# The last token row's MLP as a row of its own, and the row before it moved ahead, in a two-layer decode kernel

## The chip, the cores and the metric

The kernel runs on one core of one Trainium2 chip. The metric is the device time of one execution in microseconds. TensorE multiplies, VectorE and ScalarE move and compute, GpSimd does the reductions over partitions, SyncE (SP in the profile) issues all DMAs.

## The reference

Eight tokens (B = 8) of width D = 448 pass twice through an attention block (A) and an MLP block (B), with the same caches and weights both times:

```python
x = x + _A_ref(_layernorm(x), k_cache, v_cache, wq, wo)     # 16 query heads on 8 kv heads, Sk=4096, Dh=256
x = x + _B_ref(_layernorm(x), w1, w2, w3, w4)
x = x + _A_ref(_layernorm(x), k_cache, v_cache, wq, wo)
x = x + _B_ref(_layernorm(x), w1, w2, w3, w4)
# _A_ref: q = x @ wq; softmax(q k / 16) v per head; concatenated heads @ wo
# _B_ref: the first half shifts columns along the sequence. With one position (S = 1) its shifted
#         columns are all zero, so that half adds nothing:
#         x1 = x;  return x1 + gelu(_layernorm(x1) @ w3) @ w4,  F = 1792
```

Everything is in bfloat16. Each token row has its own K and V cache of 8 heads, 2 MB each for K and for V. One layer reads 268 MB of them; the two layers would read 537 MB, and the kernel keeps some of it on chip between the layers.

## The kernel before

**Work items.** The kernel is written as a list of operations, each with an engine, the data that it reads and writes, the PSUM banks that it uses, an estimated duration and a priority. `Plan.schedule` plays the list through a small model of the engines and fixes the order on each; `synchronise` adds the semaphore waits. Two rules of `Plan.op` matter here. An operation waits for the writers and readers of its data, and an operation that uses a bank waits for the last operations of the other engines on that bank, in the order in which the program was written. So everything that uses the shared bank `psM` keeps its written order where engines alternate. The priority is by default the place in the list; operations of `dv` and `pe` have it lowered by a million (`urge[0]` = `CH`) and so go first, unless `urge[0]` is set to 0. The planner's model of TensorE counts blocks of 128 instruction pairs (`fetched`, `BLOCK`), and fills expected idle time with dummy matmuls on the identity (`filler`, L1366 to L1377).

**Tiling.** K and V come from DRAM in quarters of 512 KB ("units"), each a slot `kv[:, slot*2048 ...]`; there are 30 slots. One DMA brings up to `most` neighbouring units (`next_kv`). It is issued when as many slots in a row are free. A K quarter is transposed on TensorE as f32 words (L1165, four 128 x 128 transposes per bank of `psT`, eight banks' worth per head) and copied back over itself by VectorE (L1148) or ScalarE (L1149).

**A head.** `front` does the 64 score matmuls of a head (L985, 16 per quarter, into `psM` columns 256 on), copies them to `sS` (L1004), finds the maximum, and takes the exponential on ScalarE (L1019) into `pT`. A K quarter's slot is free after its score matmuls. `back` loads V and multiplies `pT` with it: 32 matmuls of 128 x 2 weights against 256 columns, in four column groups of the array (L1050), into one of two banks `psP` by turns. VectorE copies the result in two bf16 parts to `oS` (L1064, L1066), four matmuls add the groups (L1074), L1080 divides by the sum into `oT`, and four matmuls with wo add the head to a row in `psR` (L1099). After a row's seventh head, that row is copied to `oW` in two parts (L1109, L1111) and turned into columns in `psM` ("turn", lines L927 and L930 of the helper `dup`), and L1123 adds x. The eighth head goes through wo directly in columns ("wo_mm", also L927 and L930), and L1135 writes the new x.

**Order of the rows.** Row b's second layer is woven with the first layer of row b + 1. Heads are kept or free: K of heads 3 to 7 stays on chip between the layers (head 7 half, the rest of it held in transposed form), V of head 7 and half of head 6. The rest is read twice. Heads 0, 1 and 2 are the free ones. The last row (b = 7) has no next row, and runs these tasks, "f" for `front` and "b" for `back`, with 6/0 for head 0 of row 6, which is finished here:

b 6/0, f 6, f 7, b 6/1, f 0, b 6, b 6/2, f 5, f 1, | b 7, f 4, f 2, b 5, f 3, b 4, b 3, b 0, b 1, b 2.

The bar is ours; the change refers to that place. After a front of the second layer the next head's query is computed (`second_queries`, L1220 and L1223, matmuls at L814), also on `psM`.

**MLPs.** `mlp` computes sums (L722) and moments, the inverse root by two Newton steps (L700 to L708), w3 as 56 matmuls (L830), gelu (L880, L891, L893, the tanh at L895 on ScalarE, L906 into `hT`), w4 as 70 matmuls in columns (`y_mm`, L927 and L930 through `dup`), and L919 adds the residual. It is used for each row's first layer, for rows 0 to 5 of the second layer together (in row 5, on a bank of `psT`), and for rows 6 and 7 of the second layer at the very end, with n = 2, on `psM`. `result` then turns the columns into rows (L1187), copies them (L1191) and writes them out (L1193).

Of the kernel before, what the change touches and what calls it, by code (L numbers as in the profile page):

```python
# [6 lines left out]
P = 128  # L7
B = 8
D = 448
# [16 lines left out]
AT = (-4, -3, -2)  # L26
MLP_ROW, MLP_AT, MLP_TO = 5, 3, 7
OUT_AT = 23.5
QLAST = 2
# [430 lines left out]
def bass_interleave_layers__gqa_block_cached__mixer_s_mlp__decode_kernel(  # L460
# [44 lines left out]
    ident_f = sb("ident_f", [P, P], f32)  # L505
    ident_b = sb("ident_b", [P, P], bf)
    xT = sb("xT", [P, NC5, B], bf)
# [4 lines left out]

    xf = sb("xf", [P, NC5, 4], bf)
    xoT = sb("xoT", [P, NC5, B], bf)
    acc = [sb(f"acc{i}", [P, NC5], f32) for i in range(2)]
# [14 lines left out]
    yb = sb("yb", [P, NC5, B], bf)  # L530
    q1T = sb("q1T", [P, B, 32], bf)
    q2T = [sb(f"q2T{i}", [P, 32], bf) for i in range(2)]
    cursor[0] = (cursor[0] + 31) // 32 * 32
# [10 lines left out]
    x_row = nc.alloc_sbuf_tensor_at("x_row", [B, NC5 * P], bf, offset=row0)  # L544
    o_row = nc.alloc_sbuf_tensor_at("o_row", [B, D], bf, offset=row0)
    assert row0 + 2 * NC5 * P <= hb0 + 4 * D
    NR, NO, NS = 6, 2, 2
# [29 lines left out]


    sems = {e: nc.alloc_semaphore(f"s_{e}") for e in ("pe", "dve", "act", "pool")}
    slot_sem = [nc.alloc_semaphore(f"s_slot{i}") for i in range(QUARTERS)]  # L580
# [55 lines left out]
    def const_a(gp):  # L636
        gp.memset(ident_f[:, :], 0.0)
        gp.memset(x_row[:, D:D + P], 0.0)
        gp.memset(mask[:, :], 1.0)
        gp.memset(x3T[:, :, :], 0.0)  # L640
        for t, c in [(t, 1) for t in x1c + x2c] + [(xf, 2)]:
            gp.memset(t[:, :, c:c + 1], 1.0)
            last = gp.memset(t[:, :, c + 1:c + 2], -1.0)
# [214 lines left out]
    WQ = ["wq0", "wq1", "wq2", "wqx0", "wqx1"]  # L858

    def mlp(src, skey, n, dst, dkeys):  # L860

# [22 lines left out]
        else:  # L884
# [11 lines left out]
                rd=["g2"], wr=["g1"], prio=urge[0] + len(plan.ops))  # L896
        for r in range(n) if few else ():

# [7 lines left out]
        dv(lambda v: v.scalar_tensor_tensor(hT[:, 0:m], a_, 1.0, h_, ALU.add, ALU.mult),  # L906
           rd=HB + ["g1"], wr=["hT"])

        def y_mm(t):
# [119 lines left out]
    def back(layer, b, h):  # L1029
# [40 lines left out]
        def sum_mm(t):  # L1070
            last = None
            for c in range(2):
                for w in range(2):
# [16 lines left out]
                             (x2c[b % 2][:, :, 0], ("x2", b),  # L1090
                              x3T[:, :, b] if b < B - 2 else xf[:, :, b - B + 2], ("x3", b)))
        ak = ("acc", layer)
# [32 lines left out]
        if k == HKV:  # L1125
            def wo_mm(t):
# [8 lines left out]
            dv(lambda v: v.tensor_tensor(xout, acc[layer][:, :], psM[:, YC:YC + NC5 * YW:YW], ALU.add),  # L1135
               rd=["psM", ak], wr=[ok] + (["x3all" if b < B - 2 else "xf"] if layer else []), banks=[M],
               name="acc", prio=hi)
# [38 lines left out]

    s_out = nc.alloc_semaphore("s_out")

    def result(n, at):
# [3 lines left out]
        def ot(t):  # L1183
            last = None
            for kc in range(4):
# [3 lines left out]
            return last  # L1189
        pe(ot, 4, rd=[("xo", at), "ident_b"], wr=[key], banks=[bk])  # L1190
        mark(dv(lambda v: v.tensor_copy(o_row[0:n, :], ps[0:n, :].bitcast(bf)[:, 0:D]), dur=0.5,  # L1191
           rd=[key], wr=["o_row", "hb", "g1", "g2", "hT"], banks=[bk]))
        plan.op("sp", lambda eng: eng.dma_start(out[at:at + n, 0, :], o_row[0:n, :]), 0.1, "out",  # L1193
                rd=["o_row", "hb", "g1", "g2", "hT"], wr=[("done", n)],
                dma=(s_out, 32 if at else 16), prio=loads[0] + (11.5 if at else OUT_AT))

# [56 lines left out]
    def first_queries():  # L1253
        def xt(t):
# [4 lines left out]
            return last  # L1259
        pe(xt, 4, rd=["xr0", "xr1", "xr2", "ident_b"], wr=["psM"], banks=[M])  # L1260
        dv(lambda v: v.tensor_copy(xT[:, :, :].rearrange("p a n -> p (a n)"),
# [79 lines left out]
    for b in range(B):  # L1341
# [23 lines left out]

    def filler(bank):  # L1366
# [5 lines left out]
        def warm(t):  # L1372
            return t.matmul(dst, ident_b[:, :], bcast(ident_b[:, 0:n // 4], 4, 1), start=True,  # L1373
                            stop=True)
        o = Op("pe", warm, (0.22 * n / 512, 0.43 * n / 512, n, 1), "warm", 0)
        o.deps[plan.writer["ident_b"]] = True
        return o  # L1377
# [5 lines left out]
    with nc.Block() as blk:  # L1383
# [48 lines left out]
```

## Time and profile before

| | |
|---|---|
| median of 3 runs | 1109.37 us (1105.71 to 1112.99) |
| the profiled execution: its span | 1109.5 us |
| TensorE busy, matmuls | 88 % of the span, 19517 |
| VectorE, ScalarE, GpSimd busy | 52 %, 26 %, 9 % |
| mean share of the 16 DMA engines, data queue | 96.9 %, 438.41 MB |
| read from HBM | 395 GB/s over the span |
| chain that ended last | PE 54 %, DMA 32 %, VectorE 4 %, "issue" 4 % |

The profiled execution is one of its own; its span, from the first to the last instruction, is all that the page gives of its time, and it is 0.1 us above the median of the runs. Matmuls are pipelined: the busy time of a matmul row is a modelled one, and a group of n matmuls that follow each other closely takes less than n times its mean. "Idle before" names what ended the engine's idle time; "issue" is idle time in which the engine waited for nothing that the profile shows. The clock is the share of full speed that TensorE was granted.

### The profile page before, as it was taken

What the parts mean: (1) busy time and instruction counts of PE and PEld (TensorE: products, weight loads), DVE (VectorE), ACT (ScalarE), POOL (GpSimd) and SP (SyncE); (2) the same over time, 40 slices, a digit from 0 to 9 for tenths busy, and PEclk for the clock granted to TensorE, in tenths of its full rate; (3) what the DMA queues carried; (4) which work ended last, traced back from release to release, by engine and by line L of the source; (5) the groups of instructions that cost most, each with busy time, mean ns of one, the idle gap of its engine ahead of it and who ended that gap; (6) DMA issues with size and microseconds to landing.
All of it is one profiled execution on the core that took longest, in us unless ns stands there. A gap on an engine that the chain in (4) does not pass through costs nothing.

```text
span 1109.5 us, 42648 instructions
## 1 busy us (share of the span) xinstructions
PE 971.3 (88%) x19517; PEld 777.4 (70%) x19517; DVE 573.0 (52%) x1782; ACT 288.1 (26%) x844; POOL 97.9 (9%) x275
## 2 busy tenths in 40 slices
PE   4889889898889887999888898898889998899987
PEld 4678657786668756786667776777557886587774
DVE  4345445555455543655555554565445655366544
ACT  1133113331224301242122321234113330243120
POOL 0000010100100101010000100101010010101010
PEclk9899989989999969999898898999899997899898
DMA  9999999999999999999999989999999999999993
GB/s 332 410 424 421 389 388 424 425 421 380 412 424 424 418 344 428 422 425 418 378 424 423 421 326 381 425 424 420 387 402 424 425 410 364 420 423 407 329 399 163
DMA packets 54099, 441.13 MB, mean 398 GB/s; under 512 B 5776, under 2 KB 8992, under 8 KB 26528
## 3 DMA queue, kind: packets, MB, share of 16 engines
q1 hardware_dynamic: 53920, 438.41, 96.9%
q8 instruction: 153, 2.51, 0.9%
q14 instruction: 26, 0.21, 0.0%
HBM read 438.38 MB, written 0.01 MB: 395 GB/s over the span
## 4 chain that ended last, share of the span: by engine, by line
PE 54%; DMA 32%; SPq 4%; issue 4%; DVE 4%; ACT 1%; POOL 0%
PE psT L1165 20%; DMA kv<-in_A_k_cache_dram 20%; PE psM L985 15%; DMA kv<-in_A_v_cache_dram 12%; PE psP L1050 8%; SPq L616 4%; PE psR L1099 3%; PE psM L814 2%; PE psM L927 1%; PE psM L930 1%; DMA w3x_sb<-in_B_w_dram 1%; PE psP L1373 1%; PE psP L1074 1%; DVE oS L1066 1%; ACT pT L1019 1%
## 5 line engine op out<-in xcount | busy, mean ns | idle before, releaser
L1165 PE MATMUL psT<-ident_f,kv 128*128 128x128 f32 x2816 | 390.2, 284 | 23.3 <-DMA kv<-in_A_k_cache_dram 21.3
L1148 DVE COPY kv<-psT 128x512 f32<-128x512 f32 x415 | 284.3, 690 | 177.5 <-PE psT L1165 171.7
L1165 PEld LDWEIGHTS psT<-ident_f,kv 128*128 128x128 f32 x2816 | 313.2, 144 | 49.0 <-DMA kv<-in_A_k_cache_dram 28.3
L1149 ACT COPY kv<-psT 128x512 f32<-128x512 f32 x321 | 186.8, 586 | 385.4 <-PE psT L1165 384.9
L1050 PE MATMUL psP<-kv,pT 128*2 128x256 bf16 x4096 | 186.9, 292 | 27.8 <-issue 13.2
L985 PEld LDWEIGHTS psM<-q2T,kv 128*128 128x128 bf16 x4096 | 127.3, 99 | 48.0 <-issue 35.1
L985 PE MATMUL psM<-q2T,kv 128*128 128x48 bf16 x4096 | 142.5, 188 | 18.2 <-issue 14.4
L985 PEld LDWEIGHTS psM<-q1T,kv 128*128 128x128 bf16 x4096 | 135.1, 97 | 18.9 <-issue 12.5
L985 PE MATMUL psM<-q1T,kv 128*128 128x48 bf16 x4096 | 143.9, 184 | 2.2 <-issue 1.2
L1050 PEld LDWEIGHTS psP<-kv,pT 128*2 128x2 bf16 x4096 | 78.5, 84 | 70.2 <-issue 25.3
L1019 ACT ACTIVATE pT<-sS,nb,fac 128x32 bf16<-128x32 f32 x128 | 52.7, 417 | 244.0 <-DVE nb L1013 244.0
L1009 POOL PARTITION_ALL_REDUCE gm<-pm x128 | 45.6, 356 | 763.1 <-DVE pm L1007 718.0
L1004 DVE COPY sS<-psM 128x64 f32<-128x64 f32 x128 | 28.6, 223 | 108.4 <-PE psM L985 105.6
L1064 DVE CAST oS<-psP 128x256 bf16<-128x256 f32 x128 | 54.0, 422 | 49.3 <-PE psP L1050 46.9
L1099 PE MATMUL psR<-wo_sb,oT 128*1 128x448 bf16 x448 | 68.6, 390 | 4.2 <-DVE oT L1080 2.3
L1023 POOL PARTITION_ALL_REDUCE Db<-rs x128 | 51.1, 399 | 213.2 <-ACT pT L1019 213.2
L1074 PE MATMUL psP<-sel,oS 128*128 128x2 bf16 x512 | 32.1, 166 | 34.6 <-DVE oS L1066 31.1
L1074 PEld LDWEIGHTS psP<-sel,oS 128*128 128x128 bf16 x512 | 25.2, 99 | 52.5 <-DVE oS L1066 43.8
L1019 ACT ACTIVATE pT<-sS,nb 128x32 bf16<-128x32 f32 x128 | 40.9, 326 | 69.6 <-DVE nb L1013 69.5
L1066 DVE TENSOR_TENSOR oS<-psP,oS 128x256 bf16<-128x256 f32 x128 | 54.1, 423 | 3.5
L814 PEld LDWEIGHTS psM<-x2c,wq_sb 128*128 128x128 bf16 x768 | 30.5, 98 | 19.4 <-issue 6.9
L814 PE MATMUL psM<-x2c,wq_sb 128*128 128x24 bf16 x768 | 36.4, 184 | 6.2 <-issue 5.3
(157 smaller groups left out, 579.1 us busy)
## 6 DMA issues: line engine op xcount, KB each, us to landing
kv<-in_A_k_cache_dram SPq DMA_DIRECT2D x72, 2048.0 KB, 20.5
kv<-in_A_v_cache_dram SPq DMA_DIRECT2D x55, 2048.0 KB, 17.2
kv<-in_A_v_cache_dram SPq DMA_DIRECT2D x121, 512.0 KB, 7.5
kv<-in_A_v_cache_dram SPq DMA_DIRECT2D x54, 1024.0 KB, 10.6
kv<-in_A_k_cache_dram SPq DMA_DIRECT2D x23, 1024.0 KB, 12.6
kv<-in_A_v_cache_dram SPq DMA_DIRECT2D x5, 1536.0 KB, 10.9
kv<-in_A_k_cache_dram SPq DMA_DIRECT2D x12, 512.0 KB, 8.1
wo_sb<-in_A_wo_dram SPq DMA_DIRECT2D x1, 3584.0 KB, 45.4
```

What stands on the lines that cost most here:

```text
L814: last = t.matmul(bank[:, at + i * step:at + i * step + copies], w, r, start=(kc == 0), stop=(kc == 3))
L985: last = t.matmul(ps[:, SB + 2 * i:SB + 2 * i + 2 * REP], a[:, c:256:2], bcast(rhs(c), REP, 1), start=(c == 0), stop=(c == 1))
L1019: return a.activation(pT[nr][:, :, :].rearrange("p i j -> p j i")[:, jj, :], sview[:, jj, :], ACT.Exp, bias=nb[nm][:, jj:jj + 1], scale=sc ...
L1023: plan.op("pool", lambda gp: gp.partition_all_reduce(Db[nr][:, :], rs[nr][:, :], P, RO.add), 0.5, "sum", rd=[("rs", nr, 0), ("rs", nr, 1)] ...
L1050: last = t.matmul(ps[g4:g4 + 2, PV0:PV0 + DH], pT[nr][:, i, :], slot_ap(q, s * 256, 256), start=(i < 4), stop=(i >= 28), skip_group_check= ...
L1064: plan.op("dve", lambda v: v.tensor_copy(oS[:, 0, :], po), 0.36, "o", rd=[("pv", par, x) for x in range(4)], wr=["oS0"], banks=[bk], prio=hi)
L1066: plan.op("dve", lambda v: v.tensor_tensor(oS[:, 1, :], po, oS[:, 0, :], ALU.subtract), 0.36, "o", rd=["oS0"] + [("pv", par, x) for x in r ...
L1074: last = t.matmul(ps[:, PV1 + 2 * c:PV1 + 2 * c + 2], oS[:, w, c:DH:2], sel[:, :], start=(w == 0), stop=(w == 1))
L1099: last = t.matmul(psR[r:r + 1, 0:D], oT[no][:, i % 2, i // 2:i // 2 + 1], wo_sb[:, a:a + D], start=(k == 1 and i < 2), stop=(k == HKV - 1 ...
L1148: return e.tensor_copy(dst, psT[bank][:, :])
L1149: return e.copy(dst, psT[bank][:, :])
L1165: last = t.transpose(psT[bank][:, s * P:(s + 1) * P], src, ident_f[:, :])
```

## The change

Six edits, of which four belong together:

- Row 6's second MLP is no longer done with row 7's at the end. It is written into the last row's list after the ninth task (`MLP_LAST` = 9, the bar in the list above), for one row, with the default priority (`urge[0] = 0`), on `psM`. Its output goes out in a DMA of its own, which SP's order puts behind all loads.
- At the end the MLP is done for row 7 alone. `xf` becomes two tiles of one row each.
- For these two rows `y_mm`, L919 and `result` are replaced by `last_row`. x is turned into a row by matmuls with the identity (`xrow`, seven matmuls, in four pieces of G = 112 on partitions 0, 32, 64 and 96). VectorE makes of it `xs` = x + its normalised value. w4 then is a product with a column of `hT` as the stationary operand and 112 columns of w4 streaming, 14 x 4 matmuls in four column groups. One VectorE operation adds half of it to `xs`, and a DMA of four pieces of 224 bytes writes the row. `xs` lies over `q1T`, which the first layer has done with.
- V of head 2 of row 7, the last load, is issued in single quarters (`most = 1`).
- The bf16 identity is no longer a copy (L651); it is a view of the f32 identity, every second bf16 element. The x transposes at the start and the filler matmuls use it.
- Three output DMAs are waited for instead of two (`s_out`).

```diff
+MLP_LAST = 9
+G = D // 4
...
-    ident_b = sb("ident_b", [P, P], bf)
+    ident_b = ident_f[:, :].bitcast(bf)[:, 1:2 * P:2]
...
-    xf = sb("xf", [P, NC5, 4], bf)
-    xoT = sb("xoT", [P, NC5, B], bf)
+    xf = [sb(f"xf{i}", [P, NC5, 3], bf) for i in range(2)]
+    xoT = sb("xoT", [P, NC5, B - 2], bf)
...
+    xs = nc.alloc_sbuf_tensor_at("xs", [P, G], f32, offset=q1T.manual_sbuf_range[0])
+    lin = sb("lin", [P, 2], f32)
+    o_last = [sb("o_last0", [P, G], bf)]
...
-    plan.op("dve", lambda v: v.tensor_copy(ident_b[:, :], ident_f[:, :]), 0.2, "const",
-            rd=["ident_f"], wr=["ident_b"])
...
+    def last_row(src, skey, ps, bank):
+        def xrow(t):
+            last = None
+            for g in range(4):
+                a = g * G
+                while a < (g + 1) * G:
+                    kc = a // P
+                    b = min((g + 1) * G, (kc + 1) * P)
+                    last = t.matmul(ps[32 * g:32 * g + 1, P + a - g * G:P + b - g * G],
+                                    src[:, kc, 0:1], ident_b[:, a - kc * P:b - kc * P], start=True,
+                                    stop=True, skip_group_check=True, tile_position=(0, 32 * g))
+                    a = b
+            return last
+        pe(xrow, 7, rd=[skey, "ident_f"], wr=["psM"], banks=[bank])
+        dv(lambda v: v.tensor_single_scalar(lin[:, 0:1], rsy[:, 0, 0:1], 1.0, ALU.add), rd=["rsy"],
+           wr=["lin0"])
+        dv(lambda v: v.tensor_tensor(lin[:, 1:2], rsy[:, 0, 0:1], minus_mean(1, 0), ALU.mult),
+           rd=["rsy", "mom"], wr=["lin1"])
+        dv(lambda v: v.tensor_scalar(xs[:, :], ps[:, P:P + G], lin[:, 0:1], lin[:, 1:2], ALU.mult,
+                                     ALU.add), 0.2, rd=["psM", "lin0", "lin1"],
+           wr=["xs", ("q1T", 0), ("q1T", 1)], banks=[bank])
+        def yrow(t):
+            last = None
+            for fc in range(14):
+                for g in range(4):
+                    last = t.matmul(ps[32 * g:32 * g + 1, 64:64 + G], hT[:, fc:fc + 1],
+                                    w4_sb[:, fc * D + g * G:fc * D + (g + 1) * G], start=(fc == 0),
+                                    stop=(fc == 13), skip_group_check=True,
+                                    tile_position=(0, 32 * g))
+            return last
+        return yrow
...
+        if yrow:
+            o_ = o_last[dst - B + 2]
+            pe(yrow, 56, rd=["hT"] + W4, wr=[kb], banks=[bk], width=G // 4)
+            ok = [("o_last", dst)] if dst < B - 1 else ["o_row", "hb", "g1", "g2", "hT"]
+            dv(lambda v: v.scalar_tensor_tensor(o_[:, :], ch[:, 64:64 + G], 0.5, xs[:, :], ALU.mult,
+                                                ALU.add), 0.2, rd=[kb, "xs"], wr=ok, banks=[bk])
+            plan.op("sp", lambda eng: eng.dma_start(
+                out[dst, 0:1, :].rearrange("o (g j) -> (o g) j", j=G), o_[0:P:32, :]), 0.1, "out",
+                rd=ok, wr=[("done", dst)], dma=(s_out, 16 * (dst - B + 4)), prio=10 ** 6 + dst)
+            return
...
+        if (layer, b, h) == (1, B - 1, free_heads[-1]):
+            most = 1
...
-            run(k + [("b", 1, b, h) for h in free_heads])
-    mlp(xf, "xf", 2, xoT[:, :, B - 2:B], [("xo", B - 2)])
-    result(2, B - 2)
+            k += [("b", 1, b, h) for h in free_heads]
+            run(k[:MLP_LAST])
+            assert done[1, B - 2] == HKV
+            urge[0] = 0
+            mlp(xf[0], ("x3", B - 2), 1, B - 2, [])
+            urge[0] = CH
+            run(k[MLP_LAST:])
+    mlp(xf[1], ("x3", B - 1), 1, B - 1, [])
...
-            eng.wait_ge(s_out, 32)
+            eng.wait_ge(s_out, 48)
```

More of the change, by code (lines that the diff above doesn't have):

```diff
@@ L545, in bass_interleave_layers__gqa_block_cached__mixer_s_mlp__decode_kernel @@
     o_row = nc.alloc_sbuf_tensor_at("o_row", [B, D], bf, offset=row0)
+    o_last.append(nc.alloc_sbuf_tensor_at("o_last1", [P, G], bf, offset=row0))
     assert row0 + 2 * NC5 * P <= hb0 + 4 * D
@@ L576, in slot_ap @@
         return kv[:, x.slot * 2048 + a:x.slot * 2048 + a + n]
+    s_out = nc.alloc_semaphore("s_out")
     sems = {e: nc.alloc_semaphore(f"s_{e}") for e in ("pe", "dve", "act", "pool")}
@@ L640, in const_a @@
         gp.memset(x3T[:, :, :], 0.0)
-        for t, c in [(t, 1) for t in x1c + x2c] + [(xf, 2)]:
-            gp.memset(t[:, :, c:c + 1], 1.0)
-            last = gp.memset(t[:, :, c + 1:c + 2], -1.0)
+        for t in x1c + x2c + xf:
+            gp.memset(t[:, :, 1:2], 1.0)
+            last = gp.memset(t[:, :, 2:3], -1.0)
         return last
@@ L896, in mlp @@
                 rd=["g2"], wr=["g1"], prio=urge[0] + len(plan.ops))
-        for r in range(n) if few else ():
+        yrow = last_row(src, skey, ch, bk) if isinstance(dst, int) else None
+        for r in range(n) if few and not yrow else ():
             bs, k = base[:, :, r], ["base"] if r == 0 else [("base", r)]
@@ L1090, in back @@
                              (x2c[b % 2][:, :, 0], ("x2", b),
-                              x3T[:, :, b] if b < B - 2 else xf[:, :, b - B + 2], ("x3", b)))
+                              x3T[:, :, b] if b < B - 2 else xf[b - B + 2][:, :, 0], ("x3", b)))
         ak = ("acc", layer)
@@ L1135, in back @@
             dv(lambda v: v.tensor_tensor(xout, acc[layer][:, :], psM[:, YC:YC + NC5 * YW:YW], ALU.add),
-               rd=["psM", ak], wr=[ok] + (["x3all" if b < B - 2 else "xf"] if layer else []), banks=[M],
+               rd=["psM", ak], wr=[ok] + (["x3all"] if layer and b < B - 2 else []), banks=[M],
                name="acc", prio=hi)
@@ L1175, in transpose_piece @@
         return bank
-    s_out = nc.alloc_semaphore("s_out")
     def result(n, at):
@@ L1189, in ot @@
             return last
-        pe(ot, 4, rd=[("xo", at), "ident_b"], wr=[key], banks=[bk])
+        pe(ot, 4, rd=[("xo", at), "ident_f"], wr=[key], banks=[bk])
         mark(dv(lambda v: v.tensor_copy(o_row[0:n, :], ps[0:n, :].bitcast(bf)[:, 0:D]), dur=0.5,
@@ L1194, in result @@
                 rd=["o_row", "hb", "g1", "g2", "hT"], wr=[("done", n)],
-                dma=(s_out, 32 if at else 16), prio=loads[0] + (11.5 if at else OUT_AT))
+                dma=(s_out, 16), prio=loads[0] + OUT_AT)
     def mid(b, heads):
@@ L1259, in xt @@
             return last
-        pe(xt, 4, rd=["xr0", "xr1", "xr2", "ident_b"], wr=["psM"], banks=[M])
+        pe(xt, 4, rd=["xr0", "xr1", "xr2", "ident_f"], wr=["psM"], banks=[M])
         dv(lambda v: v.tensor_copy(xT[:, :, :].rearrange("p a n -> p (a n)"),
@@ L1372, in warm @@
         def warm(t):
-            return t.matmul(dst, ident_b[:, :], bcast(ident_b[:, 0:n // 4], 4, 1), start=True,
+            return t.matmul(dst, ident_b, bcast(ident_b[:, 0:n // 4], 4, 1), start=True,
                             stop=True)
         o = Op("pe", warm, (0.22 * n / 512, 0.43 * n / 512, n, 1), "warm", 0)
-        o.deps[plan.writer["ident_b"]] = True
+        o.deps[plan.writer["ident_f"]] = True
         return o
```

## The prediction

> **What bounds the kernel now.** I read the slices first, then the chain that ended last, then TensorE's timeline over the last row. The page shows a kernel that is fed by its DMA queue:
>
> ```profile
> span 1109.5 us, 42648 instructions
> DMA  9999999999999999999999989999999999999993
> q1 hardware_dynamic: 53920, 438.41, 96.9%
> q8 instruction: 153, 2.51, 0.9%
> ```
>
> All 16 engines are full until the last slice, so anything done earlier pays only if it lets bytes start sooner; what comes after the last byte is paid in full. The chain of waits shows that end (start, length, what):
>
> ```profile
> 1080.63 14.52 DMA kv<-in_A_v_cache_dram
> 1095.15 0.04 issue
> 1095.19 1.04 PE psP L1050 x32
> ```
>
> The last V is issued at 1080.63 and lands at 1095.15; the tail from there to 1109.5 is 14.35 us. The q8 row has a second message. It is the instruction queue: 153 packets for TensorE's 19517 pairs of weight load and matmul, 127.6 pairs a packet. TensorE's timeline in the last row shows what a packet costs while the data queue is full (start, length, instruction, idle before):
>
> ```profile
> 1059.84 0.66 PE L1165 MATMUL psT<-ident_f,kv 128*128 128x128 f32 x4 [1.25 <-issue]
> 1066.15 0.18 PE L814 MATMUL psM<-x2c,wqx_sb 128*128 128x24 bf16 x1 [0.75 <-issue]
> 1072.36 1.68 PE L985 MATMUL psM<-q2T,kv 128*128 128x48 bf16 x61 [0.16 <-issue]
> 1078.69 0.31 PE L985 MATMUL psM<-q2T,kv 128*128 128x48 bf16 x6 [0.86 <-issue]
> 1085.17 0.40 PE L1050 MATMUL psP<-kv,pT 128*2 128x256 bf16 x4 [2.47 <-issue]
> ```
>
> Idle that nothing in the program explains, at even distances. Counted between them (length; TensorE busy and matmuls; weight loads; and so on; clock; DMA share):
>
> ```profile
> 1066.15:1072.36 6.21, 5.04 (x128) 3.94 (x128) 2.51 (x11) 2.40 (x9) 0.76 (x2) 1.00 1.01 413
> 1072.36:1078.69 6.33, 5.47 (x127) 5.35 (x127) 3.39 (x9) 2.56 (x7) 1.16 (x3) 1.00 1.00 419
> 1078.69:1085.17 6.48, 4.01 (x128) 3.11 (x127) 2.46 (x11) 1.81 (x8) 1.48 (x4) 0.98 1.02 420
> 1085.17:1094.87 9.70, 8.92 (x160) 4.71 (x160) 4.09 (x13) 0.00 (x0) 0.00 (x0) 0.84 0.76 317
> ```
>
> In the last row TensorE gets 128 pairs per 6.3 us, however idle it is. At 1085.17 the scores of all heads are done and 160 pairs remain before the last V; they end at 1094.87, just ahead of the last V's landing. DMA and TensorE finish this row together, with 0.3 us between them.
>
> **The change, part by part.** The sum starts from the profiled 1109.5 (0.1 above the median of 1109.37).
>
> *Row 6's second MLP moves into the last row: +4.2 us.* Its pairs: 4 (sums) + 56 (w3) + 7 (x as a row) + 56 (w4) = 123, nearly one packet. It is issued after nine tasks, so on psM it stands behind the second query of head 2 (1071.7) and ahead of the scores of heads 4, 2 and 3, which began at 1072.36. These wait for its last VectorE read. In a row the same chain took 4.6 us from sums (1029.75) to hT (1034.33); here it shares VectorE with up to eight evacuations of 0.69 and one head's two copies of 0.42, say 2 us. TensorE meanwhile has 24 transposes and head 5's V product (32+8), ready since 1070.4. So by 1078.7 it has run 60+7+24+40 = 131 pairs: a packet. Then w4 as a row (56 pairs, 1.5), its read (0.5), head 4's scores (64, 1.7): 120 more by 1083, and it stands until 1085.17. At that moment the program is 123 pairs behind where it was: heads 2 and 3 still have 120 score pairs. They and 8 more fill the packet to 1085.17 + 6.4 = 1091.6. There 152 pairs remain up to the seventh head's output row, against 160 at 1085.17 before. Those took 9.70 us, 3.4 of them at a granted clock of 0.5. At full clock: the rest of head 4's V product is 24 pairs, 0.7 us, so its copy to oS comes at 1092.3; the copies before (1087.62, 1089.18, 1091.20, 1092.87) came about 1.6 apart at best, so three heads on it is 1097.1; and from the last of those copies to the end of its output row it was 1.99 (1092.87 to 1094.86): 1099.1 against 1094.87, +4.2. Lower bound: 152 pairs at 0.028 us each (the 56 w3 pairs at the end took 1.42, 25 ns each, the 70 w4 pairs 2.33, 33 ns) are 4.3 us, 1095.9, +1.0. Upper bound: all 9.70 us again, 1101.3, +6.4, and 0.6 if the chain runs longer: +7. I take the middle, which rests on the head's rhythm. On SP nothing waits behind it: row 6's output is ordered behind all loads. On VectorE, evacuations queue behind xs and the last read; four psT banks buffer them, and they are counted in the 2 us. The seventh head's chain on VectorE (L1109, L1111, the turn) keeps its length and is late with it.
>
> The Trainium skill speaks against this step: its page "Runtime: NRT & Kernel Launch", section "Instruction fetch mechanics", has the fetch hidden because the sequencer issues more slowly than blocks refill. The five rows above show the opposite under a full data queue, and the measurement decides. By the page the 123 pairs would fall into idle time of TensorE and the step would cost nothing, giving the second case below.
>
> *Does it delay the last loads?* Nothing, if two dates hold. A 512 KB load into an idle queue took 3.95 us (1041.93 to 1045.88), 1.28 of them transfer by the spacing of its neighbours, so a load must be issued 2.7 us before its turn. Head 1's V has its turn at 1085.28 and head 2's at 1090.26: issue by 1082.6 and 1087.6. Head 5's V product frees four quarters at about 1076, head 4's scores four more at 1081 to 1083. Both dates are met, the first through head 5.
>
> *Last V in quarters: 0.* It would let 24 of the 32 products run before the last landing: 1.04 us becomes about 0.4, −0.65; but with TensorE four microseconds late all of V is there first. Smaller loads land 1.28 apart, four in 5.1 against 4.89 for 2 MB: +0.2 at most. Bounds −0.65 to +0.2.
>
> *The tail with one row: −2.65.* From x3 (L1135) on, the old tail reads (start, length, engine, line):
>
> ```profile
> 1098.51 0.17 DVE L1135 TENSOR_TENSOR xf<-acc,psM 128x5 bf16<-128x5 f32 x1 [0.83 <-PE psM L930]
> 1103.48 0.19 DVE L906 SCALAR_TENSOR_TENSOR hT<-g,hb 128x28 bf16<-128x28 f32 x1 [0.29 <-ACT g L895]
> 1106.06 0.17 DVE L919 SCALAR_TENSOR_TENSOR xoT<-psM,base 128x10 bf16<-128x10 f32 x1 [2.39 <-PE psM L930]
> 1106.92 0.61 PE L1187 MATMUL psM<-ident_b,xoT 128*2 128x128 bf16 x4
> 1107.58 0.38 DVE L1191 COPY o_row<-psM 2x448 bf16<-2x448 bf16 x1 [1.34 <-PE psM L1187]
> 1107.98 0.27 SPq L1193 DMA_DIRECT2D out_dram<-o_row  x1
> ```
>
> Sums to hT: 4.93 for two rows (1098.74 to 1103.67), 4.58 for one: −0.35. The new read xs (112 columns from PSUM; rows of 64 and 256 columns take 0.22 and 0.42, so about 0.27) needs seven row matmuls after hb, during the tanh; it may end after hT: +0.1 (0 to +0.3). The product: 70 pairs in 2.33 us become 56; at 25 ns and the pipe's 0.15 that is 1.55, at 33 ns 1.85: −0.8 (−0.5 to −0.95). From there to the output DMA: 1.92 us (read 0.17, fillers that TensorE must finish first, transposes, copy) become one read of 0.27 and its hand-over: −1.6 (−1.4 to −1.7). The DMA's own 1.52 us stay. Together −0.35 + 0.1 − 0.8 − 1.6 = −2.65, bounds −1.95 to −3.0.
>
> *The identity as a strided view of the f32 one: 0.* The copy L651 (0.23 at 12.19) goes away, ahead of a DMA-bound start: 0 to −0.3. The 228 filler matmuls now stream with a step of two elements. Stationary operands show no price (96 ns at L985 with a step of two, 95 to 98 for the fillers' contiguous one); a strided moving one is not in the trace. Fillers are 1% of the chain, so were they twice as long: up to +11. I take 0, nearest to the stationary rows.
>
> **Sum:** 1109.5 + 4.2 + 0 − 2.65 + 0 = 1111.05, so 1111.0. Own range: 1109.5 + 1.0 − 3.0 − 0.65 − 0.3 = 1106.6 to 1109.5 + 7 − 1.95 + 0.2 = 1114.8.
>
> **Rivals.** *Faster, 1106.4.* TensorE stood idle about 6 us between 1059.84 and 1094.87; 123 pairs at 25 ns are 3.1. If the packets come sooner, or pairs that wait on psM were not what counted, the seventh head ends at 1094.9 as before. The tail gives 2.65 and the quarters 0.4 (acc is written by 1097.24, wo_mm starts at 1097.74). For it: the idle share; against it: four packets in a row at 6.2 to 6.5. *Slower, 1117.* The scores that free K quarters are late, and the last loads miss their dates. It decides at 1082.6: if head 5's product doesn't run early (it stood until 1078.93 before, behind scores), head 1's V waits for head 4's scores, and a chain of 12 us instead of 9 puts the issue at 1085 to 1088. The queue is then empty for some 6 us: 1111 + 6. Against it: 10 to 12 us of queued data at each of these issues. *Fillers dearer:* up to 1120. *The change does not act:* the planner's priorities leave row 6's MLP to the end; against it: its row is ready at 1062.7, and three heads' scores stand behind it on psM. Then a chain of 4.6 + 1.6 + 0.3 stands in the tail once more: 1109.5 − 2.65 + 6.5 = 1113.4.
>
> **How the numbers follow.** Forecast 0.55, faster rival 0.27, slower rival 0.10, fillers 0.05, no action 0.03. A measurement of this kernel tells about 1% (11 us) from no change; its three runs lie 7.3 us apart. Nearly all cases stay inside 1%: 0.91. Slower by over 1%: 0.06 (the fillers' far end and a longer gap of the queue); faster: 0.03. The range, 1105.5 to 1115.0, holds the forecast's own and the faster rival, 0.9 below it included for the spread of the runs.
>
> **What would show it.** Right: stalls by "issue" at 128 pairs, one packet more before the last V product; scores of heads 4, 2 and 3 from about 1081 on; wo_mm at about 1102 instead of 1097.74 while the last V lands at 1095 as before; 8.3 us from x3's start to the end instead of 11.0. Wrong: wo_mm at or before 1097.7 (the packets did not bind), a last landing after 1097 (the loads were late), or fillers of more than 0.27 and 0.38 us.

## The result and the profile after

The changed kernel took 1116.59 us (median of nine runs, 1111.39 to 1120.83) against 1108.88 for the kernel before (1105.71 to 1114.07). The ratio is 1.0059 with a 95 % interval of 1.0034 to 1.0085, that is 6.5 us slower (3.8 to 9.4). The change lies within the 1 % that the forecast called no change, but the time is above the forecast 1111.0 and above the range's end at 1115.0. The profiled execution took 1116.65 us, 1.75 more than its span.

The page of the changed kernel, its span and its instruction queue:

```profile
span 1114.9 us, 42882 instructions
...
q8 instruction: 154, 2.52, 0.9%
```

That is one packet of the instruction queue more, for 106 more matmuls. The chain of waits (start, length, what) ends differently:

```profile
1088.95 3.08 issue
...
1094.87 1.88 PE psP L1103 x32
```

The last link before the tail is no longer the landing of the last V but TensorE standing for 3.08 us with nothing to wait for in the program. TensorE's timeline over that place (start, length, instruction, idle before; L1036 are scores, L1103 V products, L892 is w4 as a row, L978 is wo_mm):

```profile
1079.68 0.80 PE L892 MATMUL psM<-w_sb,hT 128*1 128x112 bf16 x49 [0.22 <-issue]
...
1085.35 1.63 PE L1036 MATMUL psM<-q2T,kv 128*128 128x48 bf16 x59 [1.53 <-issue]
...
1087.45 1.50 PE L1036 MATMUL psM<-q2T,kv 128*128 128x48 bf16 x53
1092.03 0.62 PE L1036 MATMUL psM<-q2T,kv 128*128 128x48 bf16 x11 [3.08 <-issue]
1092.58 1.02 PE L1103 MATMUL psP<-kv,pT 128*2 128x256 bf16 x16
1094.87 1.88 PE L1103 MATMUL psP<-kv,pT 128*2 128x256 bf16 x32 [1.27 <-ACT pT L1070]
...
1106.28 0.47 PE L978 MATMUL psM<-oT,wo_sb 128*128 128x12 bf16 x12
```

The stalls are at 1079.68, 1085.35 and 1092.03; the end of a stall, where the next packet's pairs begin, is called a boundary below. The scores of head 3, the last to be done, are cut by the third: 53 stand before it, 11 behind it. wo_mm starts at 1106.28 instead of 1097.74. The two stretches between the stalls, and the 6.8 us across the third (length; TensorE busy and matmuls; weight loads; VectorE; ScalarE; GpSimd; clock, DMA share, GB/s):

```profile
1079.68:1085.35 5.67, 3.82 (x129) 2.88 (x128) 1.28 (x6) 0.89 (x4) 0.35 (x1) 1.00 1.03 428
1085.35:1092.03 6.68, 3.60 (x128) 3.20 (x128) 0.84 (x4) 0.92 (x5) 1.15 (x3) 0.97 0.99 402
1091.60:1098.40 6.80, 5.10 (x72) 2.33 (x76) 2.58 (x10) 0.91 (x4) 0.76 (x2) 0.50 0.19 73
```

Each stretch between stalls has 128 pairs once more. In the second TensorE was idle for 3.1 of the 6.68 us, and from 1091.6 it had half the clock. VectorE's timeline shows what followed (L1055 copies a head's scores, L1117 a head's V product, L1162 the row with the seventh head):

```profile
1092.69 0.23 DVE L1055 COPY sS<-psM 128x64 f32<-128x64 f32 x1 [4.48 <-PE psM L1036]
...
1095.35 0.17 DVE L1076 RECIPROCAL rc<-Db 128x2 f32<-128x2 f32 x1 [1.47 <-POOL Db L1074]
1095.43 0.40 DVE L1117 CAST oS<-psP 128x256 bf16<-128x256 f32 x1
...
1097.49 0.41 DVE L1117 CAST oS<-psP 128x256 bf16<-128x256 f32 x1
...
1100.04 0.43 DVE L1117 CAST oS<-psP 128x256 bf16<-128x256 f32 x1 [0.39 <-PE psP L1103]
...
1101.61 0.42 DVE L1117 CAST oS<-psP 128x256 bf16<-128x256 f32 x1 [0.17 <-PE psP L1103]
...
1103.76 0.62 DVE L1162 CAST oW<-psR 128x448 bf16<-128x448 f32 x1 [0.76 <-PE psR L1152]
```

The first L1117 is head 4's. Its product was there at 1093.6 (1092.58 + 1.02), but on VectorE the copy is behind the reciprocal of head 3's sum. The reciprocal waits for GpSimd's sum, the sum for the exponential, and the exponential for the 11 scores behind the stall. In the kernel before the order is the same, but there the reciprocal was done first, and VectorE waited 2.31 us more for the product:

```profile
1082.43 0.22 DVE L1004 COPY sS<-psM 128x64 f32<-128x64 f32 x1 [0.26 <-PE psM L985]
...
1085.14 0.17 DVE L1025 RECIPROCAL rc<-Db 128x2 f32<-128x2 f32 x1 [1.46 <-POOL Db L1023]
1087.62 0.42 DVE L1064 CAST oS<-psP 128x256 bf16<-128x256 f32 x1 [2.31 <-PE psP L1050]
...
1092.87 0.42 DVE L1064 CAST oS<-psP 128x256 bf16<-128x256 f32 x1 [0.17 <-PE psP L1050]
```

The four copies stood at 1087.62, 1089.18, 1091.20 and 1092.87 then: the first is 7.8 us later now, the last 8.7.

The tail, on VectorE (x3, xs, output) and on TensorE (w4 as a row):

```profile
1107.05 0.17 DVE L1188 TENSOR_TENSOR xf<-acc,psM 128x5 bf16<-128x5 f32 x1 [0.88 <-PE psM L981]
...
1111.09 0.39 DVE L884 TENSOR_SCALAR xs<-psM,lin 128x112 f32<-128x112 f32 x1
1111.42 0.17 DVE L946 SCALAR_TENSOR_TENSOR hT<-g,hb 128x14 bf16<-128x14 f32 x1
1112.57 0.28 DVE L953 SCALAR_TENSOR_TENSOR o_last<-psM,xs 128x112 bf16<-128x112 f32 x1 [0.97 <-PE psM L892]
```

```profile
1111.65 0.86 PE L892 MATMUL psM<-w_sb,hT 128*1 128x112 bf16 x56 [0.64 <-DVE hT L946]
```

From x3's start to the end of the span it is 7.85 us instead of 10.99, from wo_mm's start 8.6 instead of 11.8.

### The profile page after: what moved, and what is told of

The parts are those of the page before. It is cut to its first block, busy times and chain, and to the rows that moved or that the text cites. A ratio compares the mean times of both kernels' runs of the same rounds, so it can differ in the third digit from the quotient of the medians.

```text
span 1114.9 us, 42882 instructions
## 1 busy us (share of the span) xinstructions
PE 969.6 (87%) x19623; PEld 776.7 (70%) x19623; DVE 574.9 (52%) x1796; ACT 288.9 (26%) x846; POOL 97.8 (9%) x277
## 4 chain that ended last, share of the span: by engine, by line
PE 60%; DMA 27%; DVE 6%; issue 5%; SPq 1%; ACT 1%; POOL 0%; DVEq 0%
PE psT L1218 22%; PE psM L1036 16%; DMA kv<-in_A_k_cache_dram 16%; DMA kv<-in_A_v_cache_dram 11%; PE psP L1103 10%; PE psR L1152 4%; PE psM L818 2%; PE psP L1127 1%; PE psM L978 1%; DVE oS L1119 1%; DVE oS L1117 1%; PE psM L981 1%; SPq L606 1%; ACT pT L1070 1%; PE psP L1429 1%
## 5 line engine op out<-in xcount | busy, mean ns | idle before, releaser
L1103 PE MATMUL psP<-kv,pT 128*2 128x256 bf16 x4096 | 187.8, 295 | 28.7 <-DMA kv<-in_A_v_cache_dram 13.6
L1036 PEld LDWEIGHTS psM<-q2T,kv 128*128 128x128 bf16 x4096 | 127.7, 100 | 55.5 <-issue 41.9
L1036 PE MATMUL psM<-q2T,kv 128*128 128x48 bf16 x4096 | 143.2, 188 | 23.2 <-issue 19.6
L1036 PEld LDWEIGHTS psM<-q1T,kv 128*128 128x128 bf16 x4096 | 134.2, 97 | 19.8 <-issue 14.2
L1036 PE MATMUL psM<-q1T,kv 128*128 128x48 bf16 x4096 | 143.5, 184 | 3.3 <-issue 2.7
L1103 PEld LDWEIGHTS psP<-kv,pT 128*2 128x2 bf16 x4096 | 79.7, 85 | 68.1 <-issue 22.0
L1055 DVE COPY sS<-psM 128x64 f32<-128x64 f32 x128 | 28.6, 224 | 116.1 <-PE psM L1036 113.4
L1117 DVE CAST oS<-psP 128x256 bf16<-128x256 f32 x128 | 54.0, 422 | 50.0 <-PE psP L1103 47.7
## 6 DMA issues: line engine op xcount, KB each, us to landing
kv<-in_A_v_cache_dram SPq DMA_DIRECT2D x4, 1536.0 KB, 10.4
```

The lines of the kernel that those rows point to most:

```text
L1036: last = t.matmul(ps[:, SB + 2 * i:SB + 2 * i + 2 * REP], a[:, c:256:2], bcast(rhs(c), REP, 1), start=(c == 0), stop=(c == 1))
L1103: last = t.matmul(ps[g4:g4 + 2, PV0:PV0 + DH], pT[nr][:, i, :], slot_ap(q, s * 256, 256), start=(i < 4), stop=(i >= 28), skip_group_check= ...
L1117: plan.op("dve", lambda v: v.tensor_copy(oS[:, 0, :], po), 0.36, "o", rd=[("pv", par, x) for x in range(4)], wr=["oS0"], banks=[bk], prio=hi)
```

## The experiments

**The theory** after this profile: the moved MLP costs twice. Its 123 pairs are nearly a packet, and its chain on `psM` holds back the scores of the last three heads. Together they push head 3's last scores behind one more boundary, and everything that hangs on head 3's softmax waits through the stall. **The rivals:** the pairs alone cost a packet, wherever they are; the chain alone, by its waits, makes the scores late; or the tail and the quarters, not the moved MLP, cost something.

All ratios are to the kernel before, on the same chip. Beside them stand, from the one profile of each, "row", the time from the first copy of scores in the last row to wo_mm (53.9 us before, 62.5 after), the starts of the last two heads' score copies, and the time from the start of the last of these copies to wo_mm.

| kernel | ratio (95 %) | us of 1109 | row | last two score copies | last copy to wo_mm |
|---|---|---|---|---|---|
| before | 1 | | 53.9 | 1080.1, 1082.4 | 15.31 |
| changed | 1.0059 (1.0034–1.0085) | +6.5 | 62.5 | 1087.0, 1092.7 | 13.59 |
| without the moved MLP | 0.9978 (0.9954–1.0001) | −2.4 | 55.0 | 1080.8, 1083.1 | 15.36 |
| before with 123 idle pairs | 1.0023 (0.9999–1.0047) | +2.6 | 58.1 | 1089.1, 1091.4 | 12.35 |
| chain with 33 pairs | 1.0001 (0.9977–1.0025) | +0.1 | 54.5 | 1084.0, 1086.4 | 12.30 |
| moved MLP on its own bank | 1.0042 (1.0018–1.0067) | +4.7 | 60.5 | 1090.4, 1093.1 | 11.03 |
| 108 pairs ahead | 1.0032 (1.0016–1.0048) | +3.5 | 57.2 | 1083.8, 1086.8 | 12.31 |
| 64 pairs ahead | 1.0022 (1.0001–1.0042) | +2.4 | 59.3 | 1085.8, 1090.7 | 12.31 |
| 128 pairs ahead | 1.0051 (1.0026–1.0076) | +5.7 | 57.5 | 1087.4, 1091.4 | 12.31 |
| moved MLP after head 0 | 0.9997 (0.9977–1.0017) | −0.3 | 56.1 | 1079.3, 1081.6 | 20.13 |
| both rows at the end | 1.0000 (0.9983–1.0018) | 0.0 | 53.9 | 1078.9, 1081.2 | 17.09 |
| the same, no fillers in the end | 0.9989 (0.9965–1.0013) | −1.2 | 53.2 | 1076.3, 1078.6 | 14.80 |
| after head 0, no fillers in the end | 1.0017 (0.9987–1.0047) | +1.9 | 56.1 | 1077.9, 1080.3 | 19.31 |
| before, 256 idle pairs after the last load | 1.0042 (1.0016–1.0069) | +4.7 | 59.5 | 1080.5, 1082.9 | 20.92 |

The last column shows what the rows of single profiles have in common. In five kernels it is 12.30 to 12.35: there everything up to wo_mm hangs on the last head's scores. In the kernel before it is 15.31, because wo_mm waited for the last V, so the scores had 3.0 us to spare. In the changed kernel the last copy came 10.26 us later than before (1082.43 to 1092.69). Less the 3.00 to spare, and with the 1.28 by which its 13.59 is above 12.31, these are the 8.54 us by which wo_mm is late.

**Without the moved MLP.** The changed kernel with row 6's second MLP left out; the tail, the quarters and the identity stay.

```diff
-            mlp(xf[0], ("x3", B - 2), 1, B - 2, [])
...
-            eng.wait_ge(s_out, 48)
+            eng.wait_ge(s_out, 32)
```

> The changed kernel without row 6's second MLP: that row is not computed and not written; the rest, the single row at the end and the last V in quarters too, is as changed. It sizes the moved MLP and the tail. Packet theory (TensorE gets 128 pairs of weight load and matmul per 6.3 us while the data queue is full, so 123 more pairs in the last row cost more than a packet's time) and chain theory (the scores of three heads wait on psM for the moved MLP's last read, whatever its pairs) say the same here: the last heads end as in the kernel before, the last V lands last, and the whole is 3.5 us faster than the kernel before (2.5 to 4.5). The filler theory (dummy matmuls read the identity with a step of two and are dearer) says equal or slower than before.

It is 2.4 us faster than before (−5.1 to +0.1), not quite clear of nothing. So the moved MLP costs 1.0059/0.9978, some 9 us (± 3.9, the two intervals added as the root of their squares). The rival that the other edits cost something falls: at the interval's end they cost 0.1 us.

**Pairs alone.** The kernel before, with 123 matmuls on the identity, of which nothing comes, after the last second query that stands ahead of the late scores (head 2's).

```diff
+EXTRA = 122
...
+            if (b, h) == (B - 1, free_heads[-1]):
+                for _ in range(EXTRA):
+                    t.matmul(psR[:, 448:472], ident_b[:, :], ident_b[:, 0:24], start=True, stop=True,
+                             skip_group_check=True)
+                last = t.matmul(psR[:, 448:472], ident_b[:, :], ident_b[:, 0:24], start=True, stop=True,
+                                skip_group_check=True)
```

> The kernel before, plus 123 matmuls of the w3 kind (128 x 128 weights, 24 columns) on the identity, issued right after the second query of head 2 of the last row, into a PSUM region that nobody reads. No chain, no new wait; the order of all else is the old one. Packet theory: the boundaries of packets come 123 pairs earlier in the work, the seventh head ends 5 to 8 us later, the kernel is 4 to 8 us slower than before. Chain theory: 3.1 us of TensorE time fall into some 6 us of idle time, 0 to 1 us slower.

It cost 2.6 us (−0.1 to 5.2), less than expected. A stall on TensorE, and SP's waits from 1040 to 1110:

```profile
1080.99 1.82 PE L986 MATMUL psM<-q2T,kv 128*128 128x48 bf16 x56 [2.75 <-issue]
```

```profile
engine line waited for: us in total, times, longest us
SPq L617 <- PE psM L986: 30.9, 11, 10.4
```

SP stood up to 10.4 us on scores (7.1 before), and the last V landed at 1098.99 instead of 1095.15. Here, and not in the changed kernel, the loads missed their date, as the slower rival of the prediction had it. But no product waited for them: the last copy of scores stands 12.35 us ahead of wo_mm, as in the kernels with no late load, so the late scores set the end here too. Pairs alone, then, make the scores late, but don't cost 9 us.

**The chain with few pairs.** The moved MLP keeps its whole chain, its reads and its place; only of w3 one of four contraction steps is done, and of w4 two of fourteen (so row 6 lacks part of its MLP).

```diff
-            for kc in range(4):
+            for kc in (0,) if few else range(4):
...
-            for fc in range(14):
+            for fc in (0, 13) if few else range(14):
```

> The changed kernel, with row 6's moved MLP cut to 33 pairs: w3 uses one of four row blocks (14 matmuls) and w4 two of fourteen (8), so row 6's values are wrong; its chain on VectorE and ScalarE, its waits on psM and the planned order are as changed. Packet theory: 90 fewer pairs, the stall before head 3's last scores goes away or is met earlier, 4 to 7 us of the loss come back: -2 to +3 us against the kernel before. Chain theory: nothing comes back, +5 to +8.

The loss is gone (+0.1 ± 2.7, or +2.6 ± 3.7 against the kernel without the moved MLP), though the scores are as late as the chain makes them:

```profile
1081.26 0.23 DVE L1056 COPY sS<-psM 128x64 f32<-128x64 f32 x1 [2.26 <-PE psM L1037]
...
1084.00 0.20 DVE L1056 COPY sS<-psM 128x64 f32<-128x64 f32 x1
...
1086.41 0.23 DVE L1056 COPY sS<-psM 128x64 f32<-128x64 f32 x1 [1.23 <-PE psM L1037]
```

The last copy is 4.0 us later than before (1082.43), and 3.0 of these were to spare. It is 6.3 earlier than in the changed kernel, and no score of the last two heads is behind a long stall. The chain alone, as the cause of the whole loss, falls too.

**Its own bank.** The moved MLP on a bank of `psT`, so that scores needn't wait for its reads.

```diff
...
+            i = tcount[0] % NT
+            where[0] = (psT[i], ("psT", i), ("T", i))
+            held_banks.add(i)
             mlp(xf[0], ("x3", B - 2), 1, B - 2, [])
+            held_banks.remove(i)
+            where[0] = (psM, "psM", M)
```

> The changed kernel, with w3, x as a row and w4 of the moved MLP on a bank of psT instead of psM; only its sums stay on psM, so the scores of heads 4, 2 and 3 wait for the moments' read alone. Same pairs (123). Packet theory: the scores come earlier, but the same number of pairs must pass before the last heads' V products: +4 to +8 us against the kernel before. Chain theory: scores start some 6 us sooner than in the changed kernel and the loss is gone, -3.5 to 0.

Most of the loss stays (+4.7, 2.0 to 7.4). The copy of head 4's scores moved up to 1078.84, but heads 2 and 3 came at 1090.37 and 1093.11. Its timeline shows no long stall just ahead of those two (0.55 and 0.20 us; one of 2.94 came earlier, at 1070.61, in another head's scores). Transposes of K, with one bank of `psT` less, and V products stood before them until 1089. So the run took one wait away and brought another. It shows that the loss doesn't need the moved MLP's product and its last read on `psM`, and tells nothing of the pairs.

**The place of the cut.** Idle pairs early in the program, ahead of everything in question, shift all later boundaries: `EXTRA` = 108 or 64 places the cut elsewhere, 128 (a whole packet) puts it back where it was.

```diff
+EXTRA = 108
...
+            if g == 0:
+                for _ in range(EXTRA):
+                    t.matmul(psR[:, 448:472], ident_b, ident_b[:, 0:24], start=True, stop=True,
+                             skip_group_check=True)
```

> The changed kernel with 108 matmuls that nobody reads added in the first row (some 1000 us earlier, where they hide behind the loads). All packet boundaries then fall 20 pairs later in the work of the last row; order, waits and pairs there are unchanged. In the changed kernel a boundary cut the last head's scores with 11 of 64 to go, and they stood 3.1 us. If the place of the cut is what made the step dearer than forecast, the scores of the last head finish before the stall, its exponential runs under it, and the row's last product starts 2.5 to 4 us earlier after the last landing: 2.5 to 4 us faster than the changed kernel. If only the count of pairs matters, 20 pairs are 20/128 of 6.3 us, 1.0 us faster.

> As the run with 108 added matmuls, but with 64, so that the boundaries fall 64 pairs later in the last row. Count alone: 64/128 of 6.3 us, 3.2 us faster than the changed kernel. Place of the cut: the last head's scores are done before the stall as well, so 3.5 to 5 us faster; no worse than with 20. If the loss had another cause than packets (psM, the clock alone), both runs equal the changed kernel.

> The control of the two shifted runs: the changed kernel with 128 added matmuls in the first row, one whole packet. The boundaries then fall on the same matmuls of the last row as in the changed kernel. If the place of the cut made the difference, the last head's scores are cut again with about 11 to go, and the kernel is as slow as the changed one: +5 to +8 us against the kernel before, the row's last product some 62 us after the copy of the first head's scores (62.5 in the changed kernel, 57.2 with the cut 20 later). If the added matmuls themselves brought the gain, it is as fast as with 108: +3.

With the cut as in the changed kernel the loss is +6.5 and +5.7, elsewhere +3.5 and +2.4: by the means of the ratios 1.0055 against 1.0027, some 3 us apart (± 2.5). With 108 pairs the boundary fell in a V product after all scores:

```profile
1088.10 0.39 PE L1110 MATMUL psP<-kv,pT 128*2 128x256 bf16 x7 [0.93 <-issue]
```

With 64 it did not fall as expected: 11 pairs of head 4's V product and all 64 scores of head 3 stand behind it. It came 4.7 us earlier than the one that cuts head 3's scores in the changed kernel, and the last copy 2.0 us earlier (1090.65):

```profile
1087.32 0.62 PE L1110 MATMUL psP<-kv,pT 128*2 128x256 bf16 x11 [1.74 <-issue]
1087.87 2.74 PE L1043 MATMUL psM<-q2T,kv 128*128 128x48 bf16 x64
```

With 128 it fell once more between scores 53 and 54 of head 3, as it should:

```profile
1090.86 0.45 PE L1043 MATMUL psM<-q2T,kv 128*128 128x48 bf16 x11 [1.16 <-issue]
...
1091.35 0.23 DVE L1062 COPY sS<-psM 128x64 f32<-128x64 f32 x1 [2.77 <-PE psM L1043]
...
1094.08 0.40 DVE L1124 CAST oS<-psP 128x256 bf16<-128x256 f32 x1
...
1098.98 0.42 DVE L1124 CAST oS<-psP 128x256 bf16<-128x256 f32 x1 [0.17 <-PE psP L1110]
```

but the stall in this one profile was 1.16, not 3.08, and its row 57.5, hardly longer than the 57.2 with 108 and shorter than the 59.3 with 64. The profiles of 128 and 108 are of executions faster than their medians (1114.40 against 1117.04, 1109.46 against 1114.01). So the times say that the place of the boundaries counts for some 3 us of the 9, and the single profiles don't bear it out. Nor do the runs part it from a rival in the expectations, the mere count of pairs: boundaries that fall 20 or 64 pairs later would be worth 20 or 64 of 128 parts of 6.3 us, which is 1.0 us with 108 and 3.2 with 64. Against the changed kernel the two gained 3.0 ± 3.3 and 4.1 ± 3.6. It is supported, not settled.

What these three profiles do show is the price of half the clock. Behind their last score copy they ran at full clock, and there the four copies of V products span 4.90 us each time (1094.08 to 1098.98 above), against 6.18 in the changed kernel: the 1.28 us of the last column.

**The same pairs, later.** `MLP_LAST` 17 instead of 9: the MLP is written after head 0's V product, when all scores are through.

```diff
-MLP_LAST = 9
+MLP_LAST = 17
```

> The changed kernel with row 6's MLP placed behind the back of head 0 (17 tasks instead of 9): no scores stand behind it on psM any more, only the row's turn. Same pairs. Packet theory: scores are done by 1083 as in the kernel before, but 283 pairs instead of 160 must pass between 1085 and the seventh head's row; one packet by 1091.6, the rest at the pace of the last heads: the last product starts 2.5 to 4 us later than in the kernel before, the tail gives 3.2 back: -1 to +1 us against the kernel before. Chain theory: -3.5, as without the moved MLP.

The same row with the same 123 pairs is 6.9 us (± 3.6) faster than the changed kernel and not to be told from the kernel before. It has its stalls too, but behind the last head's scores:

```profile
1084.34 0.38 PE L1103 MATMUL psP<-kv,pT 128*2 128x256 bf16 x5 [2.48 <-issue]
...
1090.38 0.91 PE L1152 MATMUL psR<-wo_sb,oT 128*1 128x448 bf16 x4 [1.80 <-issue]
```

Against the kernel without the moved MLP the pairs cost 2.1 us here (± 3.4), about what the idle pairs alone cost in the kernel before. Pairs without scores behind them cost 2.1, the chain with few pairs 2.6, both at once 9. That this is more than the sum (by 4.3 ± 5.2) is not shown by the times alone. That either one taken away gives most of the loss back is shown (6.9 ± 3.6 and 6.4 ± 3.9 faster than the changed kernel).

**Both rows at the end, as rows.** One `xf` of two rows, no moved MLP; x and w4 as rows with two columns of `hT`, five small VectorE operations for `lin`, two output DMAs.

```diff
-            mlp(xf[0], ("x3", B - 2), 1, B - 2, [])
...
-    mlp(xf[1], ("x3", B - 1), 1, B - 1, [])
+    mlp(xf, "xf", 2, B - 2, [])
...
-                                    src[:, kc, 0:1], ident_b[:, a - kc * P:b - kc * P], start=True,
+                                    src[:, kc, 0:2], ident_b[:, a - kc * P:b - kc * P], start=True,
...
-                    last = t.matmul(ps[32 * g:32 * g + 1, 64:64 + G], hT[:, fc:fc + 1],
+                    last = t.matmul(ps[32 * g:32 * g + 2, 64:64 + G], hT[:, 2 * fc:2 * fc + 2],
```

> Only the changed tail, with both rows at the end: sums, w3 and gelu for two rows as in the kernel before, then x and w4 as rows with two hT columns stationary (7 and 56 matmuls instead of 70 and 4 transposes), one read, and two output DMAs; the last V in quarters. No pair moves ahead. By the rows: w4 and the end of the tail save 2.4, five small VectorE operations and the second DMA cost 0.5 to 0.8: 1.5 to 2.5 us faster than the kernel before, and 5 to 9 faster than the changed kernel. If the tail's gain came from doing one row only, no gain.

The expectation was missed: there is no gain. Its chain of waits in the tail (start, length, what; psT L1431 are filler matmuls):

```profile
1100.56 1.66 PE psM L834 x56
1102.22 2.15 PE psT L1431 x5
1104.36 0.20 PE psM L874 x5
1104.57 0.97 PE psT L1431 x2
1105.53 1.43 PE psM L898 x52
```

From 1096.9 to 1106.1 the clock was 0.50, and the fillers, 0.43 to 0.49 us each at that clock, stand in the chain ahead of the x row and the w4 row with 3.1 us.

**No fillers in the end.** The planner places none after the last MLP begins, in the kernel with both rows at the end and in the one with the MLP after head 0.

```diff
-            if e == "pe" and self.filler and t - free["pe"] > 0.1:
+            if e == "pe" and self.filler and t - free["pe"] > 0.1 and o.idx < self.calm:
```

> The kernel with both rows at the end as rows, without the dummy matmuls that the planner puts into the final MLP's waits. In the profile of that kernel nine of them stood before the row matmuls and w4, 3.1 us of the chain at half clock. If they are what ate the tail's gain, 1.5 to 3 us faster than the kernel before. If they keep the clock up and that is worth more, equal to the kernel before or slower.

> Row 6's MLP behind the back of head 0, and no dummy matmuls in the final MLP. Its row took 2.3 us longer than the kernel before's, its tail 9.9 in the profile (8.6 in the changed kernel). Packet theory: the same 123 pairs in the last row; 0 to 1.5 us faster than the kernel before, slower than the version with both rows at the end by 1 to 2.

With both rows at the end the median ratio is 0.9989, 1.2 us below the kernel before and not clear of it; after head 0 it is 1.0017, likewise within its interval of 1. In the kernel with both rows at the end, with no fillers, TensorE stood idle from 1096.9 to 1098.3, and its clock was 0.50 from 1096.9 to the span's end at 1104.0. wo_mm started at 1093.39 there and at 1098.30 with fillers: without them the half clock begins later in the work, but does not go away. Neither kernel is shown to beat the kernel before.

**Pairs with an empty data queue.** The kernel before, with 256 idle pairs just ahead of row 7's wo_mm, when no load is left.

```diff
+                if (layer, b) == (1, B - 1):
+                    for _ in range(256):
+                        t.matmul(psR[:, 448:472], ident_b[:, :], ident_b[:, 0:24], start=True, stop=True,
+                                 skip_group_check=True)
```

> The kernel before, plus 256 matmuls of the w3 kind that nobody reads, issued just before the last product with wo, when no load is in flight any more. Two packets of instructions more, with an empty data queue. If a packet is late because it stands behind queued data, these pairs run at their own pace (25 ns each, 6.4 us; 12.8 at half clock) without an idle gap by issue: 6 to 8 us slower than before at full clock. If a packet takes 6.3 us whatever the queue, gaps of some 3 us stand between them: 12 to 13 us slower.

```profile
1097.38 6.56 PE L1130 MATMUL psR<-ident_b 128*128 128x24 bf16 x256 [0.26 <-DVE oT L1080]
```

Two packets' worth of pairs ran in 6.56 us with no gap by "issue": at most 3.3 us a packet, against 5.7 to 6.7 from boundary to boundary in the last rows of the two kernels, where the 16 engines are full. By the times it cost 4.7 us (1.8 to 7.7).

The instruction queue's own records agree. In the changed kernel its packets start at 1082.9 and 1089.5, 3.2 and 4.2 us after the boundaries at 1079.68 and 1085.35, and 2.5 us later TensorE goes on. Here packets start at 1099.1 and 1102.9; counted in pairs from the stall at 1091.67, the boundaries before them are at 1098.6 and 1101.8, so only 0.5 and 1.1 us passed. What the packets cost in the last row is thus not a constant of TensorE. That a packet waits among the data on the DMA engines fits both, and nothing else that differs between the two cases was tested.

## Why the prediction was wrong, point by point

**The base.** The sum started from the span, 1109.5, as if it were the execution's time. In the changed kernel a time is 1.75 us above its span (1116.65 against 1114.9). With as much here, the profiled execution of before took some 1111.3 us, not 0.1 above the median of the runs but 2.4 above that of nine, 1108.88. Span against span the forecast said +1.5 and the profiles show +5.4; by the times it is +6.5.

**Row 6's second MLP, +4.2: the step that failed.** It measured +8.5 at wo_mm's start (1097.74 to 1106.28), above its upper bound of 7, and some 9 by the times. The mechanism was as told: packets of 128 pairs, stalls by "issue", one packet more, late scores (copies at 1083.2, 1087.0 and 1092.7). So was the boundary, 1092.03 where the working had 1091.6. Three pieces of the working behind it were wrong.

- It let head 3's scores and eight more pairs fill that packet. In the run 16 pairs of head 4's V product ran ahead of them, and 11 scores fell behind the boundary.
- It then went on with head 4's V product and put its copy at 1092.3. It didn't name what stands ahead of this copy on VectorE, the reciprocal of head 3's sum. The copy came at 1095.43, 3.1 us late.
- It took three more heads at 1.6 each, 4.8 us, at full clock. The run needed 6.2, with half the clock from 1091.6 to 1098.4. The rhythm was right: at full clock it is 4.90 in the three kernels with pairs ahead.

With 2.10 instead of 1.99 from the last copy to the end of the output row (1103.71), 3.1 + 1.4 + 0.1 is the 4.6 by which that row missed 1099.1. The "upper bound" missed it because it took the old 9.70 us again, in which no softmax was behind the boundary.

In the terms of the table, the forecast followed the pairs behind the boundary and not the chain from the last head's scores to wo_mm, 12.3 us at full clock. In the one profile that chain, started 10.26 us later with 3.00 to spare, gives 7.26 of the 8.54 us, and the half clock 1.28. How much of the scores' lateness is the place of the cut stays open; by the times its share is 3 us ± 2.5.

The experiments agree that most of the loss takes both, the pairs and the scores behind the chain: against the kernel before, 33 pairs with the whole chain took +0.1, the 123 pairs behind the scores −0.3, both together +6.5. That both at once cost more than the sum is not shown.

**The page on fetching.** The Trainium skill, "Runtime: NRT & Kernel Launch", section "Instruction fetch mechanics", has the fetch hidden. With an empty queue the 256 idle pairs agree. Under a full data queue the measurement decides against it once more: TensorE stood at each boundary, for 1.53 and 3.08 us at the last two of the changed kernel. By the page the 123 pairs would have cost nothing; they cost 2.6 us alone (−0.1 to 5.2, not clear of nothing), and some 9 with the chain and the scores behind them.

**The last loads, 0: right.** They were issued between 1079.0 and 1082.8, and the last V landed at 1094.40 (1095.15 before). The slower rival did not come about; the kernel was slower by another way, on TensorE.

**Quarters, 0:** no run has this edit alone. The trace fits the reason given: the last V landed at 1094.40, and TensorE came to its products later, from 1101.50 on.

**The tail, −2.65:** it measured −3.1 by the traces (11.8 to 8.6), outside its bound of −3.0 by a little. From x3's start it is 7.85 where 8.3 was forecast. The parts missed both ways. From the sums to hT it took 4.20 us, where 4.58 and 0.1 had been taken. From hT to the read of the product it is 1.4 less than before, where 0.8 had been taken: w4's row took 0.86 us for 56 pairs, 15 ns each, where 25 to 33 had been taken. From that read to the end it is only 1.1 less, where 1.6 had been taken. xs took 0.39 where 0.27 had been taken. So the sum was near partly by luck.

**The strided identity, 0: right.** The fillers of the changed kernel (minimum, median and maximum in ns):

```profile
L1429 PE MATMUL psP<-ident_f x186: 272/274/408, 118.1 to 1080.6; 128*128 128x248 bf16 x186
```

Minimum and median were 266 and 269 before (and of the 512-column ones 376 and 379, now 385 and 387): 5 ns for each of 186 and 8 for each of 40 are 1.2 us of TensorE, spread over its idle time.

**The other rivals.** The faster one fails at its own sign: wo_mm is 8.5 us later, not at or before 1097.7. The change did act: row 6's MLP stands on TensorE from its sums at 1073.16 to w4's row at 1079.68, inside the last row.

## What to carry to other kernels

Where instruction packets arrive at a fixed rate, work moved into idle time of an engine is priced by the packets it takes and by what stands behind the next boundary. Find the last instruction on which a chain of other engines hangs, take that chain's length and what it has to spare (12.3 and 3.0 us here), and ask when that instruction will run now. When a step is late, follow the in-order queues of all engines from it, not the data alone: here a finished product waited for a neighbour's softmax on VectorE. The same moved work cost 6.9 us (± 3.6) less behind the last scores than ahead of them.

## What had not been expected of the hardware

From boundary to boundary, 128 pairs took 5.7 to 6.7 us in the last rows of the two kernels, with the data queue full, and at most 3.3 with it empty. Row matmuls with one weight column in four column groups took 15 ns each on average (56 in 0.86 us), though each is shown as 212 ns. The clock was 0.50 for 6.8 us around a stall of 3.08 us, and for 9.2 us in the tail of the kernel with both rows at the end, there with TensorE shown busy for 8.94 of them, fillers included.
